# First block of a spectral filter and MLP: even and odd sums on array quarters, and a second scratch for its last rows

## The chip, the cores and the metric

The kernel runs on one core of one Trainium2 chip. The metric is the device time of one execution in microseconds. Lower is better. The core has TensorE (PE, with its weight loads PEld), VectorE (DVE), ScalarE (ACT), GpSimd (POOL) and SyncE (SP, which here only issues DMAs); DMAs are issued from SP, ACT and POOL.

## The reference

Two stages in float32; the weights of the second arrive as float64 and are converted on the chip.

```python
X = np.fft.rfft(x, axis=1)                       # x: 8 batches x 3008 rows x 256 columns
y = np.fft.irfft(X * (filt_r + 1j * filt_i), n=3008, axis=1)
t = y.reshape(24064, 256)                        # tokens
h = t @ w_in                                     # 256 -> 2048
g = h * np.clip(h + 3.0, 0.0, 6.0) / 6.0
out = g @ w_out                                  # 2048 -> 256
```

## The kernel before

*The transform.* 3008 = 47 x 64. A batch goes through four kinds of products: over 47 rows to 24 residues k (`a0_unit` for batch 0, `a_unit` after), over 64 to the frequencies of a residue (`b_unit`), times the filter on DVE (`f_unit`, `y_unit`), back over 64 (`bi_unit`), and back over the 24 residues to tokens (`n_first`, `n_five`, `n_unit`). Between `bi_unit` and the last step the values cross through a scratch in DRAM, `g_tmp` (`g_d`), since residues have to move from the columns of a tile to its partitions: `g_store` writes them from POOL, and `t4_load` or `first_load` reads them into the tile `t4`. The unit of the early work is a pair of residues i; `bi_unit(0, i)` treats the two pairs i and i + 1, so four residues, and batch 0 has such units at i = 0, 2, 4, 6, 8 and 10.

*Tokens.* A row j of tokens (47 of them) and the row 64 - j are made from the same values: one is the sum, the other the difference of an even and an odd part. The tile `xn` keeps both: index 0 and 1 of its third axis.

*The MLP.* The tokens go in blocks of 512, eight steps of 256 hidden columns to a block. Block 0 takes plain products (`plain_up`, `relu`, `hswish`, `plain_down`); later blocks take seven products for eight, which need sums of weights: `w_sums` on POOL, `w_scale` on ACT. Those sums start when the 15th of the 16 weight parts is converted.

*The weights.* Each of the 16 parts of the weights is loaded as integers (`load_bits`), split by ACT (`w_abs`) and put together by six DVE instructions (`w_conv`, `w_conv_2`; `convert(n)` does n whole parts). The buffers of the raw bits are borrowed from later tiles ("o", "g", "x").

*The first block.* It holds the rows j = 6 to 1 of batch 0 and their mirrors, 282 pairs, of which 256 are the block. To begin early, its last four residues (units i = 10 and 11) don't cross the scratch: `direct` multiplies the filtered spectrum `y` by a table `direct_t` that goes from frequencies to tokens. The other twenty residues come from `t4` in `n_first`, which adds its products to the same PSUM tiles (`psn`, and `po2`, `po3` for row j = 1) and copies the result to `xn` on ACT. Rows of the last unit that can still arrive in time (i = 8) are stored by `g0_first`, only the twelve that the block needs, from ACT and SP.

*Order.* The order of instructions on each engine is written out by hand: up to `n_first` and the first conversions in straight code at the end of the kernel, then by a plan of places (`at`) in each step. An engine's queue is worked off in this order. The framework puts in the waits. DMAs issued from SP and ACT take eight completion semaphores in turn, those from POOL eight others, and a DMA waits until the one before it on its semaphore has landed.

The ends of this order, before:

```python
        first_load(KH - 3 * TC, KH - TC)
        for i in 1, 2:
            w_abs(i)
        direct(NU - 2)
        direct(NU - 1)
        bi_unit(0, NU - 2, [...])
        ...
        n_first()
        g_store(0, NU - 4)
        g_store(0, NU - 2)
        ...
        w_abs(3)
        convert(3)
```

Of the kernel before, what the change touches and what calls it, by code (L numbers as in the profile page):

```python
# [26 lines left out]
N = 3008  # L27
# [27 lines left out]
RING = 3 * PAIRS  # L55
ND = (NJ + 1) * TOK
NX = PAIRS - NJ * NA
ATOM = 2 * KH
# [20 lines left out]
def _make_tables():  # L79
# [64 lines left out]

    def first_of(x, n):
        if n < NJ:
            return np.concatenate(x)
        return np.concatenate([x[0][:NX], x[1][:NX], cs_of([x[0][NX:], x[1][NX:]])])
# [5 lines left out]
    first = np.zeros((P, NJ + 1, TOK))  # L154
    last = np.zeros((P, NJ + 1, TOK))
    direct = np.zeros((P, TC, ND))
    for k in range(KH):
        for j in range(HC):
            for (ri, hh), x in terms(k, j, rows).items():
                if j in FIRST:  # L160
                    first[hh * 64 + ri * 32 + k, FIRST.index(j)] = first_of(x, FIRST.index(j))
# [16 lines left out]
    wai = np.concatenate([t.reshape(P, -1) for t in (groups, ones, first, last)], axis=1)  # L178
    f = np.float32
# [4 lines left out]
def kernel(  # L184
# [123 lines left out]
    def w_load(i, q):  # L308
        if W_AT[i] == "g":
            t = gp.tile([P, 7, 256], FP32, name="g")  # L310
            st["rest"] = t[:, 4:7, :].rearrange("p a n -> p (a n)")
            t = t.bitcast(I32)[:, 0:4, :].rearrange("p a n -> p (a n)")
# [346 lines left out]
    def first_load(k0, k1):  # L659
        for h in range(2):  # L660
            for ri in range(2):
                p0 = h * 64 + ri * 32
                nc.sync.dma_start(t4[p0 + k0:p0 + k1, 0:NJ + 1, :],
                                  g_d[0, ds(h * HC + 1, NJ + 1), ri, k0:k1, :].rearrange("j k d -> k j d"))
# [56 lines left out]


    def direct(i):
        if "psn" not in st:
            st["psn"] = {(c, dh): (psO.tile([P, 2, 2, P], FP32, name="po%d" % (2 + dh)).rearrange("p a u m -> p (a u m)")
                                   if c else psF.tile([P, 512], FP32, name="psn", tag="f"))
                         for c in range(2) for dh in range(2)}
        for u in range(2):
            k = 2 * i + u - KH + TC
            for (c, dh), ps in st["psn"].items():  # L730
                t, n = c * NJ * TOK, (1 if c else NJ) * TOK
                nc.tensor.matmul(ps[:, 0:n], st["y", 0, i][:, u, ts(dh, P)], st["direct"][k][:, ds(t, n)],
                                 start=k == 0, stop=False, skip_group_check=True)

    def n_first():
        for (c, dh), ps in st.pop("psn").items():
            for q, j in enumerate(chunks[c][1]):
                strips(ps[:, ts(q, TOK)], t4[:, j - 1, ts(dh, P)], edges[:, FIRST.index(j), :], start=False, stop=True)
            to = xn[:, dh, :, 0:PAIRS]
            if c == 0:  # L740
                nc.scalar.activation(out=to[:, :, 0:NJ * NA].rearrange("p h (j a) -> p j h a", a=NA),
                                     in_=ps[:, 0:NJ * TOK].rearrange("p (j h a) -> p j h a", j=NJ, h=2), func=AXT.Copy)
                continue
            nc.scalar.activation(out=to[:, :, NJ * NA:], in_=ps[:, 0:2 * NX].rearrange("p (h a) -> p h a", h=2), func=AXT.Copy)
            nc.scalar.activation(out=xn[:, dh, :, ds(PAIRS, NA - NX)],
                                 in_=ps[:, 2 * NX:TOK].rearrange("p (c a) -> p c a", c=2), func=AXT.Copy)

# [232 lines left out]
    with tc.manual_schedule():  # L980
# [65 lines left out]
        st["direct"] = [last[:, ts(k, ND)] for k in range(3)] + [st["rest"][:, 0:ND]]  # L1046
        nc.sync.dma_start(st["direct"][3], direct_d[:, 3, :])
        nc.sync.dma_start(edge, wai_d[:, ds(NW, ND)])
        load_bits(4)
        turn(0)  # L1050
        for c in range(NT):
# [99 lines left out]

        at(n_at[TAIL - 2] + 1, lambda: nc.sync.dma_start(edge, wai_d[:, ds(NW + ND, ND)]))
        at(LAST * NP + 3, b12_back)
# [136 lines left out]
```

## Time and profile before

| | us |
|---|---|
| median of 3 runs (2607.19 to 2607.8) | 2607.3 |
| span of the profiled execution, first to last instruction | 2607.0 |
| PE busy | 2591.8 |
| DVE busy | 2053.9 |
| first products of batch 0 on PE | 6.6 |
| `direct` on PE | 51.2 to 59.7 |
| `n_first` on PE | 61.6 to 63.8 |
| first product of the MLP | 64.2 |
| POOL's weight sums | 120.6 to 150.2 |

Times in the profile are in us from the first instruction; a line of a timeline gives start, duration, engine, source line, operation, output tile <- input tiles, shape and count, and in brackets the idle time of that engine before it and what ended it. A float32 product shows as two MATMUL records. "L765" is the helper `strips`, which all products on halves of the array's columns go through, so tile names tell them apart. The chain of waits is followed back from the last instruction, so each of its pieces is what the next one waited for. The span stands for the profiled execution's own time; it lies 0.3 us under the median.

### The profile page before, as it was taken

The numbers are of one execution on the slowest core, as the hardware profiler recorded it, in microseconds if no ns is written. First come the engines' busy times: TensorE is split into PE (matmuls) and PEld (weight loads), VectorE is DVE, ScalarE is ACT, GpSimd is POOL, SyncE is SP. The second block draws the span as 40 slices with busy tenths as digits, with TensorE's granted clock in tenths as the row PEclk, the third lists the DMA queues.
The fourth block names the chain that finished last, engine by engine and source line by source line (L and its number), as shares of the span: only waits on it lengthen the run. The fifth ranks groups of instructions, "written<-read, shape, count | busy, mean of one in ns | idle before, by whom it ended". The sixth has DMA issues, their size and how long they took to land.

```text
span 2607.0 us, 86613 instructions
## 1 busy us (share of the span) xinstructions
PE 2591.8 (99%) x37708; PEld 2051.0 (79%) x37708; DVE 2053.9 (79%) x3611; ACT 1295.6 (50%) x2677; POOL 486.7 (19%) x711
## 2 busy tenths in 40 slices
PE   8999999999999999999999999999999999999999
PEld 6487777878778787788877888777877778888887
DVE  7978868888788877888778887788877888766666
ACT  4554454545545455444554444545445454455554
POOL 2242021121211202111031210311113120111110
PEclk9999999999999999999999999999999999999999
DMA  8732234112241132411224112331123321110000
GB/s 247 224 92 81 59 101 119 54 33 87 74 123 54 33 87 78 119 54 37 83 83 114 54 38 82 89 108 54 54 66 91 106 57 49 50 44 24 20 22 26
DMA packets 130834, 200.32 MB, mean 77 GB/s; under 512 B 21602, under 2 KB 97472, under 8 KB 130262
## 3 DMA queue, kind: packets, MB, share of 16 engines
q1 hardware_dynamic: 115165, 150.12, 20.4%
q0 software_dynamic: 14720, 44.16, 6.1%
q8 instruction: 296, 4.85, 0.8%
q14 instruction: 84, 0.69, 0.1%
q10 hardware_dynamic: 569, 0.50, 0.1%
HBM read 122.43 MB, written 83.98 MB: 79 GB/s over the span
## 4 chain that ended last, share of the span: by engine, by line
PE 94%; DVE 3%; DMA 2%; POOL 1%; issue 0%; ACT 0%; SPq 0%; POOLq 0%; DVEq 0%; ACTq 0%
PE po L765 43%; PE al L765 24%; PE be L765 18%; PE psn L705 2%; PE psf L540 1%; PE psf L481 1%; PE psf L600 1%; PE be L600 1%; POOL w_all L369 1%; PE be L481 1%; DVE g L818 1%; DMA g_tmp<-t 1%; PE psf L765 0%; DMA ft<-in_filt_i_dram 0%; DVE y L335 0%
## 5 line engine op out<-in xcount | busy, mean ns | idle before, releaser
L765 PEld LDWEIGHTS po<-w_all,g 128*64 128x64 f32 x20808 | 1232.5, 137 | 247.0 <-issue 12.4
L765 PE MATMUL po<-w_all,g 128*64 128x128 f32 (+1 forms) x20808 | 1407.0, 274 | 1.4 <-DVE g L818 0.7
L813 ACT ACTIVATE r<-h,half_c 128x512 f32<-128x512 f32 x736 | 531.0, 722 | 346.7 <-DVE h L794 334.7
L765 PE MATMUL al<-xt,w_all 128*64 128x256 f32 x4416 | 664.0, 379 | 0.4 <-POOL w_all L369 0.3
L818 DVE SCALAR_TENSOR_TENSOR g<-r,h 128x512 f32<-128x512 f32 x736 | 536.2, 730 | 144.6 <-ACT r L813 129.2
L765 PE MATMUL be<-xt,w_all 128*64 128x256 f32 x2944 | 442.6, 379 | 0.0
L794 DVE TENSOR_TENSOR h<-be,s 128x512 f32<-128x512 f32 x368 | 253.8, 690 | 131.3 <-PE be L765 102.2
L760 POOL TENSOR_TENSOR xt<-xn 128x256 f32<-128x256 f32 x184 | 150.7, 838 | 890.3 <-ACT xn L687 890.3
L765 PEld LDWEIGHTS be<-xt,w_all 128*64 128x64 f32 x2944 | 211.3, 137 | 106.5
L765 PEld LDWEIGHTS al<-xt,w_all 128*64 128x64 f32 x4416 | 278.9, 137 | 1.7 <-POOL w_all L369 1.4
L808 ACT ACTIVATE h<-al 128x256 f32<-128x256 f32 x368 | 141.4, 384 | 273.2 <-PE al L765 272.4
L826 DVE TENSOR_TENSOR g<-g 128x512 f32<-128x512 f32 x367 | 261.4, 712 | 12.6
L799 DVE TENSOR_TENSOR h<-al,s 128x256 f32<-128x256 f32 x368 | 156.0, 424 | 135.6 <-PE al L765 130.5
L789 ACT ACTIVATE s<-al 128x256 f32<-128x256 f32 x368 | 141.6, 385 | 207.2 <-PE al L765 207.1
L765 PE MATMUL al<-xn,w_all 128*64 128x256 f32 (+1 forms) x1536 | 240.1, 393 | 1.1 <-DVE g L818 0.7
L765 PE MATMUL be<-xn,w_all 128*64 128x256 f32 (+1 forms) x1536 | 236.4, 388 | 0.0
L780 ACT ACTIVATE s<-be 128x256 f32<-128x256 f32 x368 | 141.4, 384 | 170.1 <-PE be L765 170.1
L825 DVE TENSOR_TENSOR g<-g 128x256 f32<-128x256 f32 x367 | 165.5, 451 | 12.6
L779 ACT ACTIVATE s<-al 128x256 f32<-128x256 f32 x368 | 141.5, 384 | 59.1 <-PE al L765 59.1
L831 DVE TENSOR_TENSOR g<-g 128x256 f32<-128x256 f32 x367 | 161.7, 441 | 2.4
L765 PEld LDWEIGHTS be<-xn,w_all 128*64 128x64 f32 x1536 | 110.3, 137 | 62.3 <-issue 7.4
L506 POOL DMA_DIRECT2D z_tmp<-t x144 | 72.0, 508 | 321.4 <-ACT s L780 296.0
(162 smaller groups left out, 1766.6 us busy)
## 6 DMA issues: line engine op xcount, KB each, us to landing
t<-g_tmp SPq DMA_DIRECT2D x184, 120.0 KB
t<-z_tmp SPq DMA_DIRECT2D x42, 512.0 KB
g_tmp<-t POOLq DMA_DIRECT2D x68, 256.0 KB, 4.3
z_tmp<-t POOLq DMA_DIRECT2D x120, 144.0 KB, 3.7
o_tmp<-o SPq DMA_DIRECT2D x46, 256.0 KB
xs<-in_x_dram SPq DMA_DIRECT2D x60, 192.0 KB
ft<-in_filt_r_dram SPq DMA_DIRECT2D x168, 64.0 KB
ft<-in_filt_i_dram SPq DMA_DIRECT2D x168, 64.0 KB
```

The lines of the kernel that those rows point to most:

```text
L760: nc.gpsimd.tensor_tensor(out=o, in0=x0, in1=x1, op=op_)
L765: nc.tensor.matmul(ps[ds(o, STRIP)], w[:, ds(o, STRIP)], x, skip_group_check=True, **kw)
L779: nc.scalar.activation(out=s[:, 0, :], in_=al, func=AXT.Copy)
L780: nc.scalar.activation(out=s5, in_=be[:, 1, :], func=AXT.Copy)
L789: nc.scalar.activation(out=s[:, 1, :], in_=al, func=AXT.Copy)
L794: nc.vector.tensor_tensor(out=st["h"][0].rearrange("p (a n) -> p a n", a=2), in0=be, in1=s, op=ALU.add)
L799: nc.vector.tensor_tensor(out=st["h"][1][:, 256:512], in0=al, in1=s5, op=ALU.add)
L813: nc.scalar.activation(out=r, in_=st["h"][i], func=AXT.Relu, bias=half_c, scale=1.0 / 6.0)
L818: nc.vector.scalar_tensor_tensor(out=st["g", k, p][:, o:o + 2, :].rearrange("p a n -> p (a n)"), in0=st["r", i], scalar=1.0, in1=st["h"][i ...
L825: v.tensor_tensor(out=g[:, G1, :], in0=g[:, G3, :], in1=g[:, G22, :], op=ALU.add)
L826: v.tensor_tensor(out=g[:, G3:G2 + 1:2, :], in0=g[:, G3:G1 + 1, :], in1=g[:, G11:G11 + 1, :].broadcast_to([P, 2, 256]), op=ALU.subtract)
L831: nc.vector.tensor_tensor(out=g[:, G4, :], in0=g[:, G12, :], in1=g[:, G2, :], op=ALU.subtract)
```

## The change

1. *Even and odd sums.* `direct` and `n_first` no longer compute both rows of a pair. A new helper `quarters` issues four products, for two halves of the rows (c: cosine and sine part) and two halves of the weight columns (g), each on 64 x 64 of the array. The cosine half gives the even part and goes to `psn`, the sine half the odd part and goes to `po2` or `po3`. The tables shrink to 282 columns for a residue and one table of 64 rows (`groups`, also used by `n_five`). After the products ACT copies the even part to `xn`, DVE adds and subtracts the odd part (two instructions of 128 x 256 for each half of the columns), and ACT copies the 26 pairs that belong to the next block.
2. *A second scratch.* The units i = 4, 6 and 8 are stored whole into `gf_tmp` (`gf_d`) by `gf_store`, from ACT, in halves of 64 rows (256 KB each), beside the store into `g_tmp` from POOL that stays. `gf_load` reads the rows of four residues with four DMAs of 24 KB; the twelve for three units stand together on SP after the loop. `first_load` fetches only the first eight residues, and `g0_first` goes. Unit 8's `g_store` stays behind `n_first` in the code.
3. *Order.* One conversion stands ahead of `n_first` and two behind it, where three stood behind it. The direct table is one load, and its last part no longer sits in a borrowed "g" buffer. Only the part of `t4` in use is cleared. The table reload in `wai_load` is two DMAs.

```diff
...
-            if j > 1:
+            if j:
...
-                    th = [2 * np.pi * ((fr * rows(j, h, a)) % N) / N for h in range(2)]
-                    direct[q, k - KH + TC, n * TOK:(n + 1) * TOK] = 2 / N * first_of(np.cos(th), n)
-                    direct[HALF + q, k - KH + TC, n * TOK:(n + 1) * TOK] = -2 / N * first_of(np.sin(th), n)
+                    th = 2 * np.pi * ((fr * rows(j, 0, a)) % N) / N
+                    direct[q, k - KH + TC, n * NA:(n + 1) * NA] = 2 / N * np.cos(th)
+                    direct[HALF + q, k - KH + TC, n * NA:(n + 1) * NA] = 2 / N * np.sin(th)
...
+    gf_d = nc.dram_tensor("gf_tmp", (3, NC, 2, TC, D), FP32, kind="Internal").ap()
...
-    def g0_first(i):
+    def gf_store(i):
         t = st["t3", 0, i]
         for v in range(2):
-            for h in range(2):
-                (nc.scalar, nc.sync)[v].dma_start(g_d[0, ds(h * HC + 1, NJ + 1), :, ds(2 * (i + v), 2), :].rearrange("c ri u d -> c ri (u d)"),
-                                    t[ds(v * 64 + h * HC + 1, NJ + 1)].rearrange("p ri u d -> p ri (u d)"))
+            nc.scalar.dma_start(gf_d[i // 2 - 2, :, :, ds(2 * v, 2), :].rearrange("c ri u d -> c ri (u d)"),
+                                t[ts(v, 64)].rearrange("p ri u d -> p ri (u d)"))
+
+    def gf_load(i, qs):
+        for h in range(2):
+            for ri in range(2):
+                qs[h].dma_start(t4[ds(ri * HALF + h * KH + 2 * i, TC), 0:NJ + 1, :],
+                                gf_d[i // 2 - 2, ds(h * HC + 1, NJ + 1), ri, :, :].rearrange("j k d -> k j d"))
...
+    def quarters(ps, dh, w, x, **kw):
+        for g in range(2):
+            for c in range(2):
+                nc.tensor.matmul(ps(c, dh)[ts(g, HALF)], w(c, ds(dh * P + g * HALF, HALF)), x(c), **kw)
...
-            for (c, dh), ps in st["psn"].items():
-                t, n = c * NJ * TOK, (1 if c else NJ) * TOK
-                nc.tensor.matmul(ps[:, 0:n], st["y", 0, i][:, u, ts(dh, P)], st["direct"][k][:, ds(t, n)],
-                                 start=k == 0, stop=False, skip_group_check=True)
+            for dh in range(2):
+                quarters(lambda c, dh: ps[c][dh][:, 0:NE], dh, lambda c, m: y[ts(c, HALF), u, m],
+                         lambda c: st["direct"][ts(c, HALF), ts(k, NE)], start=k == 0, stop=False, skip_group_check=True)
 
     def n_first():
-        for (c, dh), ps in st.pop("psn").items():
-            for q, j in enumerate(chunks[c][1]):
-                strips(ps[:, ts(q, TOK)], t4[:, j - 1, ts(dh, P)], edges[:, FIRST.index(j), :], start=False, stop=True)
-            to = xn[:, dh, :, 0:PAIRS]
...
+        ps = st.pop("psn")
+        for dh in range(2):
+            for q, j in enumerate(FIRST):
+                quarters(lambda c, dh: ps[c][dh][:, ts(q, NA)], dh, lambda c, m: t4[ds(c * HALF, ATOM), j - 1, m],
+                         lambda c: groups[ds(c * HALF, ATOM), j, :], start=False, stop=True, skip_group_check=True)
+            e, o = (xn[:, dh, c, :] for c in range(2))
+            odd = ps[1][dh]
+            nc.scalar.activation(out=e[:, 0:NE], in_=ps[0][dh][:, 0:NE], func=AXT.Copy)
+            nc.vector.tensor_tensor(out=o[:, 0:PAIRS], in0=e[:, 0:PAIRS], in1=odd[:, 0:PAIRS], op=ALU.add)
+            nc.vector.tensor_tensor(out=e[:, 0:PAIRS], in0=e[:, 0:PAIRS], in1=odd[:, 0:PAIRS], op=ALU.subtract)
+            nc.scalar.activation(out=o[:, PAIRS:NE], in_=odd[:, PAIRS:NE], func=AXT.Copy)
...
-        nc.gpsimd.memset(t4, 0.0)
+        nc.gpsimd.memset(t4[:, 0:NJ + 1, :], 0.0)
...
-        last = x0_at(HC * D - 2048, 3 * ND)
-        nc.sync.dma_start(last, direct_d[:, 0:3, :].rearrange("p k n -> p (k n)"))
+        st["direct"] = x0_at(HC * D - 2048, TC * NE)
+        nc.sync.dma_start(st["direct"], direct_d.rearrange("p k n -> p (k n)"))
+        nc.sync.dma_start(wai[:, NA:NA + NE], wai_d[:, NA:NA + NE])
         load_bits(3)
...
             if c:
                 bi_unit(0, 2 * c - 2)
-                (g0_first if c == NT - 1 else lambda i: g_store(0, i))(2 * c - 2)
-            if c == 4:
-                first_load(0, KH - 3 * TC)
-        first_load(KH - 3 * TC, KH - TC)
+            if c == NT - 2:
+                first_load(0, KH - 4 * TC)
+            if c > 2:
+                gf_store(2 * c - 2)
+            if 0 < c < NT - 1:
+                g_store(0, 2 * c - 2)
+        gf_load(NU - 8, (nc.sync, nc.sync))
+        gf_load(NU - 6, (nc.sync, nc.sync))
+        gf_load(NU - 4, (nc.sync, nc.sync))
...
+        convert(1)
         n_first()
...
-        convert(3)
+        convert(2)
...
-            nc.sync.dma_start(wai, wai_d[:, 0:NW])
+            for n0, n1 in (0, NA), (NA + NE, NW):
+                nc.sync.dma_start(wai[:, n0:n1], wai_d[:, n0:n1])
...
```

More of the change, by code (lines that the diff above doesn't have):

```diff
@@ L56 @@
 ND = (NJ + 1) * TOK
+NE = (NJ + 1) * NA
 NX = PAIRS - NJ * NA
@@ L143, in cs_of @@
         return np.concatenate([(x[0] + x[1]) / 2, (x[1] - x[0]) / 2])
[L145 to L148, printed above, removed]
     rows = np.vectorize(row, excluded=(0, 1))
@@ L153, in _make_tables @@
     ones = np.zeros((P, 2, TOK))
-    first = np.zeros((P, NJ + 1, TOK))
     last = np.zeros((P, NJ + 1, TOK))
-    direct = np.zeros((P, TC, ND))
+    direct = np.zeros((P, TC, NE))
     for k in range(KH):
@@ L159, in _make_tables @@
             for (ri, hh), x in terms(k, j, rows).items():
-                if j in FIRST:
-                    first[hh * 64 + ri * 32 + k, FIRST.index(j)] = first_of(x, FIRST.index(j))
                 if j < 2:
@@ L174, in _make_tables @@
                 for n, j in enumerate(FIRST):
-                    th = [2 * np.pi * ((fr * rows(j, h, a)) % N) / N for h in range(2)]
-                    direct[q, k - KH + TC, n * TOK:(n + 1) * TOK] = 2 / N * first_of(np.cos(th), n)
-                    direct[HALF + q, k - KH + TC, n * TOK:(n + 1) * TOK] = -2 / N * first_of(np.sin(th), n)
-    wai = np.concatenate([t.reshape(P, -1) for t in (groups, ones, first, last)], axis=1)
+                    th = 2 * np.pi * ((fr * rows(j, 0, a)) % N) / N
+                    direct[q, k - KH + TC, n * NA:(n + 1) * NA] = 2 / N * np.cos(th)
+                    direct[HALF + q, k - KH + TC, n * NA:(n + 1) * NA] = 2 / N * np.sin(th)
+    wai = np.concatenate([t.reshape(P, -1) for t in (groups, ones, last)], axis=1)
     f = np.float32
@@ L310, in w_load @@
             t = gp.tile([P, 7, 256], FP32, name="g")
-            st["rest"] = t[:, 4:7, :].rearrange("p a n -> p (a n)")
             t = t.bitcast(I32)[:, 0:4, :].rearrange("p a n -> p (a n)")
@@ L661, in first_load @@
             for ri in range(2):
-                p0 = h * 64 + ri * 32
+                p0 = ri * HALF + h * KH
                 nc.sync.dma_start(t4[p0 + k0:p0 + k1, 0:NJ + 1, :],
@@ L720, in n_unit @@
             ready(i)
+    def quarters(ps, dh, w, x, **kw):
+        for g in range(2):
+            for c in range(2):
+                nc.tensor.matmul(ps(c, dh)[ts(g, HALF)], w(c, ds(dh * P + g * HALF, HALF)), x(c), **kw)
     def direct(i):
         if "psn" not in st:
-            st["psn"] = {(c, dh): (psO.tile([P, 2, 2, P], FP32, name="po%d" % (2 + dh)).rearrange("p a u m -> p (a u m)")
-                                   if c else psF.tile([P, 512], FP32, name="psn", tag="f"))
-                         for c in range(2) for dh in range(2)}
+            st["psn"] = [[psO.tile([P, 2, 2, P], FP32, name="po%d" % (2 + dh)).rearrange("p a u m -> p (a u m)")
+                          if c else psF.tile([P, 512], FP32, name="psn", tag="f") for dh in range(2)] for c in range(2)]
+        ps = st["psn"]
+        y = st["y", 0, i]
@@ L735, in n_first @@
     def n_first():
-        for (c, dh), ps in st.pop("psn").items():
-            for q, j in enumerate(chunks[c][1]):
-                strips(ps[:, ts(q, TOK)], t4[:, j - 1, ts(dh, P)], edges[:, FIRST.index(j), :], start=False, stop=True)
-            to = xn[:, dh, :, 0:PAIRS]
[L740 to L746, printed above, removed]
+        ps = st.pop("psn")
@@ L1039 @@
             convert(j == 4)
-        nc.gpsimd.memset(t4, 0.0)
+        nc.gpsimd.memset(t4[:, 0:NJ + 1, :], 0.0)
         for c in range(FB, NT):
             table_load(0, c)
-        last = x0_at(HC * D - 2048, 3 * ND)
-        nc.sync.dma_start(last, direct_d[:, 0:3, :].rearrange("p k n -> p (k n)"))
+        st["direct"] = x0_at(HC * D - 2048, TC * NE)
+        nc.sync.dma_start(st["direct"], direct_d.rearrange("p k n -> p (k n)"))
+        nc.sync.dma_start(wai[:, NA:NA + NE], wai_d[:, NA:NA + NE])
         load_bits(3)
-        st["direct"] = [last[:, ts(k, ND)] for k in range(3)] + [st["rest"][:, 0:ND]]
-        nc.sync.dma_start(st["direct"][3], direct_d[:, 3, :])
-        nc.sync.dma_start(edge, wai_d[:, ds(NW, ND)])
         load_bits(4)
@@ L1150, in places @@
             return a_at, f_at, y_at, bi_at
-        at(n_at[TAIL - 2] + 1, lambda: nc.sync.dma_start(edge, wai_d[:, ds(NW + ND, ND)]))
+        at(n_at[TAIL - 2] + 1, lambda: nc.sync.dma_start(edge, wai_d[:, ds(NW, ND)]))
         at(LAST * NP + 3, b12_back)
```

## The prediction

> **What bounds the kernel now.** I read the page's parts 1 and 4 first, then the chain of waits near the start, because every line of the diff works in the first 80 us.
>
> ```profile
> span 2607.0 us, 86613 instructions
> PE 2591.8 (99%) x37708; PEld 2051.0 (79%) x37708; DVE 2053.9 (79%) x3611; ACT 1295.6 (50%) x2677; POOL 486.7 (19%) x711
> PE 94%; DVE 3%; DMA 2%; POOL 1%; issue 0%; ACT 0%; SPq 0%; POOLq 0%; DVEq 0%; ACTq 0%
> ```
>
> PE is the bound of the kernel as a whole. The 3% of DVE and the DMA and POOL shares are the first 140 us, and only there can the change act. The chain between 49 and 70 us:
>
> ```profile
> 50.98 4.56 DMA g_tmp<-t
> 55.56 2.31 DMA g_tmp<-t
> 58.19 3.34 DMA t<-g_tmp
> 61.62 1.86 PE psn L765 x40
> 64.22 1.94 PE al L765 x8
> 68.64 0.69 DVE g L818
> 69.33 0.35 DVE y L333
> ```
>
> The end of the transform for the first block is a chain of small DMAs: rows are stored, a second store waits for the first, they are loaded again, and `n_first` starts on PE when the load has landed, at 61.6. From 68.64 on the chain is DVE. DVE's timeline shows why:
>
> ```profile
> 63.60 0.43 DVE L337 TENSOR_SCALAR y<-y 128x512 int32<-128x512 int32 x1
> 65.64 0.69 DVE L354 TENSOR_TENSOR y<-g,y 128x512 f32<-128x512 f32 x1 [1.61 <-ACT g L324]
> 67.81 0.69 DVE L818 SCALAR_TENSOR_TENSOR g<-r,al 128x512 f32<-128x512 f32 x1
> 69.24 0.42 DVE L333 TENSOR_SCALAR y<-xt 128x512 int32<-128x512 int32 x1
> 119.77 0.69 DVE L361 SCALAR_TENSOR_TENSOR w_all<-s,y 128x512 f32<-128x512 f32 x1
> 120.95 0.69 DVE L818 SCALAR_TENSOR_TENSOR g<-r,al 128x512 f32<-128x512 f32 x1 [0.49 <-ACT r L813]
> ```
>
> No row of DVE between 65.64 and 119.77 carries an idle note: it converts weights and makes the first block's activations back to back. What hangs on its end is POOL's run of weight sums, and PE waits for those:
>
> ```profile
> 120.61 29.57 POOL L369 TENSOR_TENSOR w_all<-w_all 128x128 f32<-128x128 f32 x51 [15.89 <-DVE w_all L361]
> 139.46 0.65 PE L765 MATMUL al<-xt,w_all 128*64 128x256 f32 x4 [0.28 <-POOL w_all L369]
> ```
>
> So one mark decides: the conversion that DVE begins at 69.24, after the first two activations. What moves it moves POOL's start at 120.6 and PE at 139.5 by as much. An earlier PE alone gains nothing.
>
> **The change part by part.** *Products on quarters.* `direct` now issues 32 products of 64 rows, 64 columns of weights and 282 moving columns, where it issued 16 on the whole array:
>
> ```profile
> 51.16 1.81 PE L732 MATMUL psn<-w_all,t 128*128 128x470 f32 x4 [1.02 <-ACT t L587]
> 59.22 0.58 PE L732 MATMUL po<-g,t 128*128 128x94 f32 x4
> 95.15 1.38 PE L705 MATMUL psn<-wai,t 48*64 48x47 f32 x80
> ```
>
> Before, they take 51.16 to 59.7, 8.5 us. The four 470-column records follow each other in 1.6 us, two products, so 282 columns take 0.48. The third row is the same quarter form in `n_five`: ten groups of four products in 1.31 us, 0.13 for a group of 47 columns, so the four do run side by side. Eight groups cost 3.9 us; side by side not at all, 15.4. This gain of 4.6 us I cost at nothing: unit 11 of the spectrum is ready on DVE only at 54.65, so `direct` ends near 56.7, the last inverse products (1.1 us, 59.73 to 60.8 before) near 57.9, and then `n_first` waits for its loads.
>
> *The loads of `n_first`*, whose landing I call L (61.5 before). By the order of the built program:
> - `gf_store(4)` goes from ACT at 42.4 (the copy before POOL's store at 42.65). The eight completion semaphores of SP's and ACT's DMAs are taken in turn, and each DMA waits for the one before it on its semaphore. The direct table (issued at 36.6 before) and its neighbour on SP now wait for the two halves of `gf_store(4)`, and two weight loads of 512 KB stand behind them. So 1.75 MB that moved before 48.5 now start near 46. The table is needed at 51.2; lands near 50, hidden; ACT's second weight split needs its load by 58, hidden too.
> - `gf_store(8)` goes from ACT when both copies of unit 8 are done: 50.9 in both kernels, since PE runs without a gap up to these products. The copies used to wait until 49.8 for a store to land (longest wait of ACT on DMA 1.9 us) but PE ends the products only at 50.1. It stores 2 x 256 KB, where the old kernel stored 4 x 24 KB. ACT took 0.74 to 1.34 us for an issue, so the second half starts near 52. POOL's own store of unit 8, 512 KB, which waited until 62, goes at the same time.
> - Landing of such 256 KB stores: the rows issued at 33, 38, 42 and 48 took 4.8, 8.3, 6.3 and 3.7 us (least 2.9, most 9.7). DMA is busy with the delayed loads, so I take 5.4, between the last two: 57.4. Bounds 54.9 and 61.7.
> - The fourth row load of `gf_load(4)` waits on the semaphore of the first half, and all eight of `gf_load(6)` and `gf_load(8)` come after the second half on the one queue: seven more issues at 0.49 (four took 2.05) give 60.8. Landing 2.31 (the lone 24 KB store at 55.56) to 3.34 (the load at 58.19): L = 63.6. Bounds 60.3 and 68.6.
>
> *From L to the mark.* PE starts 0.09 after L (61.53 to 61.62); six groups of 0.13 for the first half, 0.79; ACT 0.24 behind (62.45 to 62.69) copies 282 columns, 0.41 between the 0.38 of 256 and the 0.57 of 470. Then DVE adds and subtracts, 128x256 with PSUM, 0.42 each (L799) at a step of 0.46: 2.5 us after L. ACT's small copy of the tail waits for that subtract, and the second half's large copy stands behind it in ACT's queue: 0.1 and 0.41, then two more on DVE: 3.9 after L. Only then come the two conversions that the change put behind `n_first`: 54.68, 58.52, 62.36 are the starts of three before, 3.84 each, so 7.68; then the two activations, 0.60 each. The mark is at L + 12.77.
>
> Before `n_first` DVE now has one conversion, 54.68 to 58.5, and stands still until L + 1.6, 6.7 us; the old order filled that with conversion and lost 1.61. The mark moves from 69.24 to 63.6 + 12.77 = 76.37, 7.1 later. Bounds with L: +3.8 and +12.1. Even with all rows there when PE is free at 57.9 it would be +1.4, since the four sums and the wait between them outweigh the 1.61.
>
> *Small parts.* The clearing of `t4` halves on POOL at 7 us, long before use; one DMA more in the table reload, about 0.4 us of SP at 72, and its rows are read by `n_five` at 95; the sums for the tail use the same table size. Nothing, covered by those distances. ACT's two issues of 1.0 after 42.4 push the copy at 44.15 by 0.3; PE needs it at 46.28.
>
> *An idle PE.* PE now stands for some 5.6 us before `n_first` and about 4.6 before the second step, since that waits for the first activation. The first matmuls of the kernel were slow:
>
> ```profile
> 3.02 3.78 PE L1028 MATMUL al<-r 128*128 128x512 f32 x4 [3.02 <-ACT r L1022]
> ```
>
> 0.95 for a record of 512 columns, when later ones follow at 0.43. Between 10 and 2600 us no gap is longer than about 1 us, so nothing shows whether it comes back. Bounds: nothing, and half speed for the first half of `n_first` (+0.8) and for the second step (about +1.5 past DVE's slack). I take nothing.
> The Trainium skill, "TensorE: Matmul & The Clock Gate", Part 1, says that PE falls to half its clock after an idle window of about 3.4 us and needs as long to come back; the granted clock in the profile is 1.00 even in 2.5 to 6.5 us, so that column would not show it. By the rule the sum would be some 1 to 2 us higher, as an estimate.
>
> *Sum.* Span 2607.0 + 7.1 = 2614.1; the profiled execution lies 0.3 below the median 2607.3, so 2614.4.
>
> **The rivals.** *A, likeliest:* as summed, L between 61.7 and 66, +5.2 to +9.5: 2612.5 to 2616.8. For it: three rings of 0.5 to 1.75 MB at the moment of the last store. Chance 0.53.
> *B, not slower:* the last store lands fast and L is below 61.7, where the shift falls under 0.2% (5.2 us, about what a measurement here tells from no change). The mechanism is the delayed loads: if they are through by 51, the store takes 2.9 to 3.7, L is 60.3 to 61.1, and the time 2611.1 to 2611.9. It decides at a landing before 55.5. For it: 1.75 MB at the 350 to 430 GB/s of 40 to 48 us need 4.5 us, about 46 to 51. Against it: another 2 MB of stores share that time. Chance 0.22.
> *C, dearer:* the store takes over 7 us, or PE restarts slowly: +9.5 to +14, 2616.8 to 2621.3. For it: the 8.3 at 38 us and the slow first records. Chance 0.21.
> *D, the quarters don't run side by side:* `direct` ends near 63.5, which L hides, and `n_first` takes 3.7 instead of 1.6, +1 to +2: inside A and C. Against it: the `n_five` row.
> *E, faster:* something later in the kernel gains, by a new rotation of the DMA semaphores. PE idles only some 6.5 us in all after 200 us. Chance 0.04.
>
> **How the numbers follow.** The prediction is A, 2614.4. The range takes A, the upper half of B and the near part of C: 2610.0 to 2619.0, leaving about 0.2. Slower by over 0.2%: A and C, 0.74; within: B, 0.22; faster: 0.04.
>
> **What would show it.** Right: DVE idle 5 to 8 us before the first of four new 128x256 sums, `n_first` on PE at 62 to 66, the direct table's load issued near 46 instead of 36.6, and POOL's sums starting at 124 to 131 instead of 120.6. Wrong: row loads landed before 60, DVE's conversions with a gap of their own that absorbs the shift, or POOL's start unmoved.

## The result and the profile after

The changed kernel takes 2626.3 us (median of 4 runs, 2623.9 to 2627.7) against 2607.6 for the old one beside it. The ratio is 1.0070, 95% interval 1.0056 to 1.0084: 18.7 us slower, where 7.1 were predicted. A second series, the last of the experiments below, gave 2624.9 us and 1.0064 (1.005 to 1.0077).

The page of the changed kernel: span, busy times, and the shares of the chain that ended last.

```profile
span 2623.4 us, 86795 instructions
PE 2591.5 (99%) x37788; PEld 2052.5 (78%) x37788; DVE 2055.2 (78%) x3615; ACT 1294.2 (49%) x2675; POOL 485.8 (19%) x711
PE 96%; DMA 2%; DVE 1%; issue 0%; SPq 0%; ACT 0%; ACTq 0%; POOL 0%; POOLq 0%; DVEq 0%
```

PE is busy for as long as before (2591.8), so the 16.4 us by which the span grew are time in which PE stands still. POOL has left the chain: its weight sums are no longer what PE waits for. The chain of waits of the changed kernel between 43 and 73 us (start, duration, what; "SPq" and "ACTq" are issues on those queues) shows where the first wait comes from:

```profile
43.76 0.58 ACTq L617
44.38 7.94 DMA gf_tmp<-t
52.33 0.32 SPq L1048
52.70 1.80 SPq L310
54.55 0.96 SPq L310
55.75 7.65 DMA t<-g_tmp
63.42 0.24 SPq L623
...
67.04 3.52 DMA t<-gf_tmp
70.65 0.41 PE psn L724 x2
```

Read it from the top. ACT issues the two halves of unit 4's scratch store; the second lands after 7.94 us, at 52.33. Only then does SP issue its small edge load (L1048) and, behind it, two weight loads of 512 KB (L310). Only behind these does `first_load` go, at 55.75, and it takes 7.65 us beside them. On the row loads of `gf_load(4)` SP waits 2.2 us for the second weight load to land and then for `first_load`, so it sends the third of them only at 63.42; the other row loads stand behind these, and the last one that PE waits for lands at 70.56, 9.0 us later than the rows before (61.53). The last scratch store, of unit 8, which the prediction took for the deciding one, is not in the chain at all.

The timeline of the same kernel on DVE, PE and POOL (in brackets the idle time before, and what ended it):

```profile
72.93 0.42 DVE L747 TENSOR_TENSOR xn<-xn,po 128x256 f32<-128x256 f32 x1 [12.96 <-ACT xn L746]
82.81 0.68 DVE L821 SCALAR_TENSOR_TENSOR g<-r,al 128x512 f32<-128x512 f32 x1
84.00 0.42 DVE L326 TENSOR_SCALAR y<-xt 128x512 int32<-128x512 int32 x1
73.95 3.68 PE L768 MATMUL al<-xn,w_all 128*64 128x512 f32 x8 [0.22 <-DVE xn L748]
83.54 2.44 PE L768 MATMUL al<-xn,w_all 128*64 128x512 f32 x8 [3.94 <-DVE g L821]
92.17 1.89 PE L768 MATMUL al<-xn,w_all 128*64 128x512 f32 x8
136.62 37.37 POOL L362 TENSOR_TENSOR w_all<-w_all 128x128 f32<-128x128 f32 x64 [15.17 <-DVE w_all L354]
```

DVE stands still for 12.96 us before the first sum, with two conversions still to do (75.2 to 82.8), and PE's second step waits 3.94 us for the activation behind them. The three PE rows are the first products of steps one, two and three. The same eight records take 3.68, 2.44 and 1.89 us. The windows of the changed kernel say why (start and end, length, busy time of PE, PEld, DVE, ACT and POOL with their counts, granted clock of PE, where 1.00 is full speed, DMA share, GB/s):

```profile
60.00:64.00 4.00, 0.00 (x0) 0.00 (x0) 0.00 (x0) 2.17 (x4) 1.12 (x2) 1.00 0.70 245
64.00:66.00 2.00, 0.00 (x0) 0.00 (x0) 0.00 (x0) 0.00 (x0) 0.01 (x1) 0.59 0.96 235
70.00:74.00 4.00, 3.13 (x98) 3.01 (x99) 0.84 (x2) 0.51 (x3) 0.00 (x0) 0.50 1.08 364
74.00:78.00 4.00, 4.00 (x10) 1.25 (x12) 3.41 (x7) 2.04 (x6) 0.00 (x0) 0.50 1.01 237
...
84.00:88.00 4.00, 4.00 (x14) 1.26 (x12) 3.76 (x8) 0.92 (x2) 0.00 (x0) 0.60 0.10 18
```

PE's clock falls to half while PE waits, and stays there until 78. It falls once more at the second step (0.60 in 84 to 88).

A better mark than the prediction's is the **third step**: the start of the last of the three PE rows, 92.17 against 75.49 before. In the old kernel the second and the third step start so:

```profile
68.55 1.94 PE L765 MATMUL al<-xn,w_all 128*64 128x512 f32 x8 [0.68 <-DVE g L818]
75.49 1.89 PE L765 MATMUL al<-xn,w_all 128*64 128x512 f32 x8
```

From the third step to the end of the span is 2530.9 to 2531.8 us in all fourteen profiled executions of this study, so whatever moves the third step moves the end, and nothing after it matters. The 16.7 us by which it is later, in three stretches:

| stretch | before | after | later by | predicted |
|---|---|---|---|---|
| start to landing of the rows | 61.53 | 70.56 | 9.0 | 2.1 |
| landing to second step on PE | 7.02 | 12.98 | 6.0 | 5.1 |
| second to third step | 6.94 | 8.63 | 1.7 | 0 |

(The predicted 5.1 is that of landing to the conversion at 69.24, 7.71 before and 12.77 foretold; DVE starts it 0.69 us after the second step in the old kernel and 0.46 after it in the changed one.) Some 1.4 of the 9.0 is already there when the spectrum starts: the first filter products are at 29.02 instead of 27.65 us. That moves from one execution to the next: 27.65, 27.73 and 28.32 in three kernels with the old products, 27.74 to 29.83 in ten with the new ones (an eleventh, with 30.91, has two loads moved to the start), 29.83 in the second profile of this same kernel. No run here separates what of it belongs to the change.

### The profile page after: what moved, and what is told of

Its sections match the earlier page's. It is cut to its first block, busy times and chain, and to the rows that moved or that the text cites. A ratio compares the mean times of both kernels' runs of the same rounds, so it can differ in the third digit from the quotient of the medians.

```text
span 2623.4 us, 86795 instructions
## 1 busy us (share of the span) xinstructions
PE 2591.5 (99%) x37788; PEld 2052.5 (78%) x37788; DVE 2055.2 (78%) x3615; ACT 1294.2 (49%) x2675; POOL 485.8 (19%) x711
## 4 chain that ended last, share of the span: by engine, by line
PE 96%; DMA 2%; DVE 1%; issue 0%; SPq 0%; ACT 0%; ACTq 0%; POOL 0%; POOLq 0%; DVEq 0%
PE po L768 44%; PE al L768 25%; PE be L768 18%; PE psn L703 2%; PE psf L533 1%; PE psf L474 1%; PE psf L593 1%; PE be L593 1%; PE be L474 1%; DMA ft<-in_filt_i_dram 0%; PE psf L768 0%; DMA wa<-wb_t 0%; PE psf L447 0%; DMA w_all<-in_x_dram 0%; DMA gf_tmp<-t 0%; DMA t<-g_tmp 0%
```

## The experiments

Two theories stood at the start. **Queue** (S in the expectations): the rows are late because SP's edge and weight loads wait for unit 4's store and the row loads stand behind them. **Last store** (W): the prediction's, the landing of unit 8's store sets the rows. Beside them, two smaller costs: the order of the conversions, and the slow PE.

**The old way of the rows, with the new products.**

```diff
-            if c == NT - 2:
-                first_load(0, KH - 4 * TC)
-            if c > 2:
-                gf_store(2 * c - 2)
-            if 0 < c < NT - 1:
-                g_store(0, 2 * c - 2)
-        gf_load(NU - 8, (nc.sync, nc.sync))
-        gf_load(NU - 6, (nc.sync, nc.sync))
-        gf_load(NU - 4, (nc.sync, nc.sync))
+                (g0_first if c == NT - 1 else lambda i: g_store(0, i))(2 * c - 2)
+            if c == 4:
+                first_load(0, KH - 3 * TC)
+        first_load(KH - 3 * TC, KH - TC)
```

> Changed kernel with the old way of the rows: no scratch of 64-row halves; units 4 and 6 go to the table by POOL's store and are loaded from there, the last unit by the four small stores, so nothing ahead on SP waits for a store from ACT. The products on quarters, the four sums on DVE and the order of the conversions stay as changed. Theory S (the direct table and the weight loads wait on SP for the second half of the scratch store of unit 4, and the row loads queue behind them): the landing of n_first's rows comes back from 70.6 to 61.5-63 us, the conversion that starts at 84.0 starts near 74-76, and the time falls from 2626 to 2613-2617, 5 to 10 us over the old kernel. What is then left is the order of the conversions (about 5) and what a waiting PE loses (1 to 2). Theory 'not the loads' (the cost sits in the sums and the slow PE alone): 2622 or more. The prediction's own rival W (the store of unit 8 alone sets the landing) also expects the low time here; the POOL run tells S from W.

Measured: 2614.1 us (10 runs), ratio 1.0022 (1.0012 to 1.0031). The rows land at 60.59, the third step is at 81.06, 5.6 later than before. So 11 to 12 of the 17 to 19 us belong to the new way of the rows, and about 6 to the new products with their order.

**The other half alone: the old kernel with the new way of the rows** (its layout of `t4` kept).

```diff
-                (g0_first if c == NT - 1 else lambda i: g_store(0, i))(2 * c - 2)
-            if c == 4:
-                first_load(0, KH - 3 * TC)
-        first_load(KH - 3 * TC, KH - TC)
+            if c == NT - 2:
+                first_load(0, KH - 4 * TC)
+            if c > 2:
+                gf_store(2 * c - 2)
+            if 0 < c < NT - 1:
+                g_store(0, 2 * c - 2)
+        gf_load(NU - 8, (nc.sync, nc.sync))
+        gf_load(NU - 6, (nc.sync, nc.sync))
+        gf_load(NU - 4, (nc.sync, nc.sync))
```

> Old kernel with only the way of the rows changed: three units' rows through the scratch of 64-row halves, loaded on SP; products on the whole array, no sums on DVE, and the old order of conversions (two ahead of n_first, one behind). The other half of the change alone. If the loads and the order of the conversions are separate costs, the rows land near 69 to 71 here too, DVE has converted two weights by then and has one left, and the third step on PE comes 13.96 us after the landing as before (75.49 against 61.53) plus 0.7 to 2.5 for a slow PE: 84 to 87, 8.5 to 11.5 later than before, time 2616.5 to 2619.5. If the products on quarters are what makes the rows late or PE slow: 2612 or less.

Measured: 2621.2 us, ratio 1.0051 (1.0037 to 1.0064), third step at 88.53: 13.3 us slower, some 2 more than the upper end expected. Its timeline on PE:

```profile
61.13 1.84 PE L738 MATMUL psn<-g,t 128*128 128x470 f32 x4 [0.48 <-DMA g<-direct_t]
73.12 3.40 PE L771 MATMUL psn<-wai,t 128*64 128x94 f32 x40 [8.71 <-DMA xt<-in_moe_w_in_dram]
```

The old direct tables are twice the size, 846 and 282 KB instead of one of 564, and they stand in the same delayed queue: `direct` itself now waits for its second table until 61.1, and `n_first` starts at 73.1, 2.5 us later than in the changed kernel. (The weight load in the last bracket is the profile's inference; `n_first` reads no weight bits, and what it waits for are the rows.) The halves 6.0 (old loads) and 13.3 (new loads alone) add up to 19.3 against 17.2 to 18.7 for both. The two costs are separate to within 2 us; that the smaller table takes a little off the queue's cost would fit the rest, but was not tested.

**The scratch stores from POOL instead of ACT.**

```diff
-            nc.scalar.dma_start(gf_d[i // 2 - 2, :, :, ds(2 * v, 2), :].rearrange("c ri u d -> c ri (u d)"),
+            nc.gpsimd.dma_start(gf_d[i // 2 - 2, :, :, ds(2 * v, 2), :].rearrange("c ri u d -> c ri (u d)"),
```

> Changed kernel with the stores to the scratch issued by POOL instead of ACT; same bytes, same loads from the scratch, same products and order. The direct table's load and the two weight loads on SP then wait for no store and are issued near 37-40 us again instead of 46.9-54.6. Theory S (what made n_first's rows late is SP's queue standing behind the store of unit 4): rows land near 62-65 instead of 70.6, time 2616 to 2620. Theory W (the landing of the last whole-unit store, unit 8, sets it, as the prediction had it): rows land at 68 or later, time 2624 to 2628.

Measured: 2616.3 us, ratio 1.0033 (1.002 to 1.0046), rows at 63.46, third step at 84.80. The chain of waits of this kernel:

```profile
52.75 0.53 POOL gf_tmp L617
53.28 5.16 DMA gf_tmp<-t
58.50 0.24 SPq L623
...
59.50 3.97 DMA t<-gf_tmp
63.55 0.31 PE po L724
```

This is the chain that the prediction had: the store of unit 8, landed after 5.16 us (predicted 5.4), then the row loads. Its numbers fit too, rows at 63.46 (63.6) and time 2616.3 (2614.4). In this kernel the last store is the limit, but with the stores on ACT the queue stands above it. The theory "last store" expected no change here and falls for the changed kernel.

**Only the two weight loads taken out of SP's queue.** First from the start of the queue on POOL:

```diff
-        load_bits(3)
-        load_bits(4)
+        load_bits(3, nc.gpsimd)
+        load_bits(4, nc.gpsimd)
```

> Changed kernel with only the two 512 KB weight loads moved from SP's queue to POOL's; the stores to the scratch stay on ACT, and the direct table's load and the 226-column edge load still wait on SP for the store of unit 4. Theory S in its narrow form (SP's queue order): the first row load follows the edge load at 52.6 instead of 55.75 us, and the two loads no longer share the DMA engines with it (they go near 40), so the rows land 3 to 6 us earlier than 70.6: 64.5 to 67.5, time 2626 - 3 to 6 = 2620 to 2623. If the delay came from the stores' bytes and not from the queue: rows at 70 or later, 2625 or more.

Measured: 2625.7 us, but with 2621.8 to 2627.4 in four runs; inconclusive as a time. In the profiled execution (2621.8) the rows land at 67.62. POOL issues the two loads at 8.2 and 9.1 us there, beside the loads that start the kernel, and the first filter products slip to 30.91, 1.9 us behind the changed kernel's. A second version has the two loads behind POOL's first store:

```diff
+            if c == 2:
+                load_bits(3, nc.gpsimd)
+                load_bits(4, nc.gpsimd)
             if c == NT - 2:
```

> As the run with the two weight loads on POOL, but issued there behind POOL's first store, near 35 to 37 us, so that they no longer share the DMA engines with the start (where the first run's table landed 1.9 us late, at 30.8 instead of 28.9). By SP's queue order the first row load goes 3 us earlier against the table's landing, and the rows land 4.8 us earlier, as in that run: near 66, time 2626 - 3.5 to 5.5 = 2620.5 to 2622.5. If the queue order isn't it, the rows land at 70 and the time stays at 2625 to 2627.

Measured: 2620.3 us (2618.8 to 2623.4), ratio 1.0050 (1.0037 to 1.0062), against 2624.9 for the changed kernel in the same series: 4.7 us. The chain of waits of this kernel:

```profile
47.17 0.52 ACTq L617
47.72 8.20 DMA gf_tmp<-t
55.93 4.01 DMA t<-gf_tmp
59.96 0.29 SPq L623
...
60.98 3.00 DMA t<-gf_tmp
```

`first_load` goes at 48.6 instead of 55.8, and the store that decides is the next one, unit 6's, landing after 8.2 us. The rows land at 63.99, 6.6 us earlier, with an early start of the spectrum (27.74) in part of it. Same stores, same engine, same bytes from the scratch: what was taken away is what stood in SP's queue. The two weight loads also ran earlier here, so the run does not separate their place in the queue from the share of the DMA engines that they took beside `first_load`.

**All conversions ahead of `n_first`.**

```diff
-        convert(1)
+        w_abs(3)
+        convert(3)
         n_first()
...
-        w_abs(3)
-        convert(2)
```

> Changed kernel with the third weight split and all three conversions ahead of n_first on DVE's and ACT's lists, so that DVE converts while it waits for the rows. By the prediction's sum, two conversions of 3.84 us stand behind n_first; if they fill the 13 us that DVE stands still, the rows land at 70.6 as before, and the first activation comes at n_first's end: the mark that was at 84.0 comes 5 us earlier or more, unless the xt buffers or ACT's splits hold it. Time 2626 - 3 to 5 = 2621 to 2623. If the order isn't it (the sums of POOL wait for something else): 2625 to 2627.

Measured: 2619.0 us, ratio 1.0043 (1.0028 to 1.0058): 6 to 7 us faster than the changed kernel, more than the 3 to 5 expected. The rows land at 69.54, 1.0 earlier, which is the earlier start of this execution (27.79 against 29.02). The landing to the second step is 8.53 instead of 12.98. The size was off because the mark was: I had counted to the conversion on DVE (84.00 to 79.61), while the second step on PE no longer waits for any activation (it starts at 78.07) and the third then waits 0.63 for DVE.

**A PE that is kept at work.** Products that serve nothing, 25 ahead of `n_first` and 11 after the first step's; `filler(n)` issues n products of 128 rows and 256 columns into a PSUM tile that nobody reads:

```diff
+        filler(25)
         n_first()
...
             if k == 0:
                 plain_up(p)
+                if p == 0:
+                    filler(11)
```

> Changed kernel with products on PE that serve nothing: 25 of 256 columns ahead of n_first and 11 after the first step's products, so that PE works through most of the two waits (11.6 us and 3.9 us). The rows still land near 70.5. Theory 'a waiting PE comes back slow' (granted clock 0.60 in 62-79 us, records of the second step 2.44 and 2.91 us where they took 1.72 before): n_first's part shortens by 0.7, the second step by 1.7, time 2626 - 2 to 2.5 = 2623.5 to 2624. If the slow records have another cause, such as transfers: no change, 2625 to 2627.5.

Measured: 2622.6 us, ratio 1.0057 (1.0042 to 1.0072), 2.3 to 3.7 faster. A window of this kernel, with the columns as above:

```profile
62.00:79.00 17.00, 15.21 (x152) 10.21 (x151) 6.51 (x13) 4.24 (x10) 1.12 (x2) 0.90 0.79 214
```

The second step in its timeline on PE:

```profile
82.51 1.94 PE L768 MATMUL al<-xn,w_all 128*64 128x512 f32 x8
84.28 1.89 PE L768 MATMUL be<-xn,w_all 128*64 128x512 f32 x8
```

The clock is 0.90 in 62 to 79 us where the changed kernel has 0.60, and the second to the third step takes 6.94 us, as in the old kernel, instead of 8.63. From landing to ACT's first copy it is 1.35 instead of 1.95. (This execution also starts 1.1 us earlier, at 27.88, which is no part of these two stretches.) So the slow PE is the clock, not transfers, and it costs 1.7 + 0.6. The transfers still ran beside it (214 GB/s in that window).

**What the new products cost at their best.** Old way of the rows, two conversions ahead and one behind, the third weight's split early, and 11 products that serve nothing behind `n_first`:

```diff
-        for i in 1, 2:
+        for i in 1, 2, 3:
             w_abs(i)
...
-        convert(1)
+        convert(2)
         n_first()
+        filler(11)
...
-        w_abs(3)
-        convert(2)
+        convert(1)
```

> Changed products with the old loads, an order that suits the four sums, and a PE kept busy: two conversions ahead of n_first and one behind it, the split of the third weight ahead of the last unit's copies, and 11 products of 256 columns that serve nothing between n_first and the first step. DVE: conversions 54.7 to 62.5, sums to 65, one conversion to 69, activations; the mark at 70 to 70.5 against 69.24 before, the third step on PE near 76.6 against 75.49. Time 1 to 2 us over the old kernel: 2609 to 2610. If the PE still slows (granted clock below 1.00 in 62 to 79 us): 2611 to 2612. At 2614, no better than the old loads alone, the order and the clock would not be the rest of the loss. Below 2607 the quarters would have a gain of their own.

Measured: 2610.5 us (11 runs), ratio 1.0009 (1.0001 to 1.0018), third step at 77.94, granted clock 1.00 throughout. The mark on DVE is at 71.66, not 70 to 70.5, with a spectrum that starts 1.6 later than before in this execution (29.25). That is as near to the old kernel as the new products came: the time that PE saves in `direct` buys nothing, since DVE has the four sums on top of its conversions and is the one that PE waits for before the second step (0.72 us).

**The old kernel with the early split alone**, so that DVE loses the only idle time that its profile showed between 65.6 and 119.8 (1.61 us):

```diff
-        for i in 1, 2:
+        for i in 1, 2, 3:
             w_abs(i)
...
-        w_abs(3)
         convert(3)
```

> Old kernel with ACT's split of the third weight moved ahead of the last unit's copies, so that DVE loses its 1.61 us wait at 65.6 (released by that split). The first activation then waits for ACT's copy of PE's first product, 66.9 instead of 67.8, and the second for the second, 68.5 instead of 68.6: gain 0.1 to 1.0 us, time 2607 to 2608, not to be told from the old kernel.

Measured: 2608.5 us, ratio 1.0003 (0.9994 to 1.0012), third step at 74.61: no difference that can be told. No run of this study beats the old kernel.

**All three costs mended, the change's own scratch kept.** Stores from POOL, two conversions ahead and one behind, fillers of 17 and 11 products:

```diff
-            nc.scalar.dma_start(gf_d[...
+            nc.gpsimd.dma_start(gf_d[...
...
-        for i in 1, 2:
+        for i in 1, 2, 3:
             w_abs(i)
...
-        convert(1)
+        convert(2)
+        filler(17)
         n_first()
+        filler(11)
...
-        w_abs(3)
-        convert(2)
+        convert(1)
```

> The changed kernel with its own scratch kept and all three costs mended: stores to the scratch from POOL (rows near 63.5), two conversions ahead of n_first and one behind with the third weight's split early, and products that serve nothing ahead of n_first (17) and behind it (11) so that PE's granted clock stays at 1.00. DVE: sums 65 to 68, conversion to 71.7, mark near 73, third step on PE near 79.4 against 75.49 before. Time 2610.5 to 2613. If the three causes are the whole loss, it is 13 to 15 us under the changed kernel; if a fourth is at work, it stays at 2615 or more.

Measured: 2617.7 us, 5 more than expected and no better than the stores on POOL alone. The fault was in the fillers, as the chain of waits shows:

```profile
58.63 7.54 PE po L1036 x34
66.17 0.18 PE psn L724
...
67.71 4.95 PE po L1036 x22
72.66 1.87 PE al L768 x8
```

Seventeen products are 34 records and take 7.54 us, 0.44 a product: I had sized them by the record. They held `n_first` and then the first step back. With 8 and 5 instead:

```diff
-        filler(17)
+        filler(8)
         n_first()
-        filler(11)
+        filler(5)
```

> As the run with all three costs mended, but with 8 products that serve nothing ahead of n_first and 5 behind it. There one of them took 0.44 us, not the 0.22 they were sized by, so that 17 of them held n_first back to 66.2 us and 11 held the first step back to 72.7, some 2.7 us each. Now 3.5 us and 2.2 us: n_first starts when the rows land, near 63.5, the first step at 68, the activations end DVE's work at 73, third step on PE near 79.5 to 80.5. Time 2611 to 2613, which leaves 3 to 5 us of the 17 to 18.7; at 2616 or more, the three causes are not the whole loss.

Measured: 2612.1 us (11 runs), ratio 1.0015 (1.0006 to 1.0024), third step at 77.70. The timeline of DVE in this kernel:

```profile
62.66 0.69 DVE L354 SCALAR_TENSOR_TENSOR w_all<-s,y 128x512 f32<-128x512 f32 x1
63.98 0.42 DVE L747 TENSOR_TENSOR xn<-xn,po 128x256 f32<-128x256 f32 x1 [0.63 <-ACT xn L746]
65.47 0.42 DVE L747 TENSOR_TENSOR xn<-xn,po 128x256 f32<-128x256 f32 x1 [0.62 <-ACT xn L746]
70.03 0.68 DVE L821 SCALAR_TENSOR_TENSOR g<-r,al 128x512 f32<-128x512 f32 x1
```

The 12.96 us of idle time are down to 0.63. Three causes, the queue, the order and the clock, are together 13 to 14 of the 17 to 19 us. Alone, the stores on POOL, the order and the fillers took off 8.6 to 10.0, 5.9 to 7.3 and 2.3 to 3.7 us, more in sum than together, so their gains overlap. The 4 that stay were not taken apart; the four sums are still on DVE's path, with two waits of 0.6 us for ACT between them.

**The changed kernel once more.**

> The changed kernel once more, beside the others on the same chip: how far its rows' landing (70.6) and its start (28.9) move from one profiled execution to the next. 2624 to 2628; landing 69 to 71.5.

Measured: 2624.9 us (2624.0 to 2625.9). The landing is at 71.19, the third step at 92.48; the first filter products at 29.83. The chain runs through the same unit 4 store (7.95 us) and the same weight loads; here the row loads wait for the second of them (8.92 us) and not for `first_load`.

## Why the prediction was right and wrong

*Right: the direction and the place.* The kernel is slower, the loss lies before the third step, and it comes from DVE and PE standing still until the rows land and from two conversions behind `n_first`. Rivals "not slower" and "faster" did not come.

*Right: the products on quarters.* The groups of four in the second unit's `direct` follow each other at 0.24 us a record, 0.48 a product, as estimated, so they do run side by side, and the rival that they don't falls. That the gain on PE is worth nothing held in the best version too.

*Right: landing to mark.* Predicted 12.77 us, measured 13.44 in the changed kernel (0.6 to 0.7 of it the slow clock, below), 12.60 with the old loads and 13.17 with the stores on POOL. The order and the sums were sized well.

*Wrong, at no cost to the number: the path behind the mark.* The prediction led it through POOL's weight sums to PE at 139.5. POOL's start did move, from 120.61 to 136.62, but in the changed kernel PE no longer waits for POOL, where it waited 0.28 us before: the path goes from the first activation straight to PE's second and third step.

*Wrong: the landing, 63.6 predicted and 70.56 measured; this is 7.0 of the miss, of which up to 1.4 is the later start of the spectrum.* The step that failed is "1.75 MB that moved before 48.5 now start near 46", and with it that the rows' landing was led through unit 8's store alone. The waits were the right ones, but I let them all end near 46, 3.6 us after the store's issue. Unit 4's first half did land at 46.8, and the table's load went at 46.89. The second half took 7.94 us, so the edge load and the two weight loads went only from 52.33 on. In that stretch, among stores above all, the DMA engines moved only 179 GB/s while 0.81 busy:

```profile
44.00:50.00 6.00, 6.00 (x31) 3.59 (x31) 5.22 (x8) 2.28 (x4) 2.26 (x4) 1.00 0.81 179
```

My own list had 4.8, 8.3, 6.3 and 3.7 us for such stores; I weighed it for unit 8 alone and let unit 4 have the shortest. I then asked only whether the table and the weights would arrive in time for their users, not what stands behind them on SP. `first_load` does, and `gf_load(4)` waits for it. So the chain to the rows went through SP's queue, not through unit 8's store; that one also went later than I had it (53.53 against 50.9), since ACT waited 4.03 us for an earlier store before its copies, and had still landed before it was needed. The upper bound of 68.6 was too low for the same reason: it stretched the last store and left the queue out. (From their own terms the two bounds come to 60.6 and 68.5 instead of 60.3 and 68.6, which changes nothing.)
The Trainium skill, "DMA: Bandwidth & Descriptors", "Anatomy of one DMA — SWDGE (gpsimd) path", says in passing that DMA engines do not wait on semaphores and that any such wait stands on the issuing sequencer. This trace agrees: between the table's load (46.89) and the edge load (52.33) SP, the issuing engine here, issues nothing. So a wait on SP has to be priced by everything that stands behind it, not by its own user alone.

*Wrong: the idle PE taken as nothing.* I had PE's two waits at 5.6 and 4.6 us; they were 11.6 and 3.9. Its slow restart cost 0.6 to 0.7 in `n_first` and 1.7 at the second step, 2.4 in all, near the sum of the two bounds that I gave (0.8 and 1.5). The filler run shows it to be the clock. My remark that the granted clock's column would not show it was wrong; it shows 0.50.
The Trainium skill, "TensorE: Matmul & The Clock Gate", "Part 1: The HAM clock gate", has half clock after an idle window of about 3.4 us and full clock after a busy one; the estimate of 1 to 2 us that I worked out from it and set aside was nearer than my nothing. The drop in the changed kernel, 5.3 us after PE's last product, fits that rule; its way back, 7.4 us after work had begun, is longer than such a window. The run with the old loads does not: there waits of 1.62 and 0.28 us were enough (last section), and the measurement decides.

*Wrong: where the profiled execution stands.* I put it 0.3 us under the median by taking the span for its time. In most runs shown here the time is 1.7 to 2.0 us above the span, so the execution with a span of 2607.0 took about 2608.8 and lay 1.3 over the median, while the one of the changed kernel (2625.5) lay 0.8 under its own. The 0.3 in the sum rested on this reading and was small; but the two executions together make 2.1 us by which the medians differ more than the two profiles do, and that is scatter, no mechanism.

*Together*: 7.0 for the landing, 2.4 for the clock and 2.1 for the two executions are 11.5 of the 11.9 us by which the time was missed. The signs went the foretold way and too far: DVE idle for 12.96 us instead of 5 to 8, `n_first` at 70.65 instead of 62 to 66, POOL's sums at 136.62 instead of 124 to 131; only the table's load, at 46.89, was where it was put. Rival C named a slow store and a slow PE, but had the slow store at unit 8, and its +14 is short of the 18.7 measured.

## What to carry to other kernels

When a moved store makes a load wait, list everything that stands behind that load on its queue, and follow the latest of the store's pieces, not the first. Price stores by the rate that stores show in the same stretch, not by that of loads. And where a change makes PE wait for more than a microsecond or two, add the half clock behind the wait, or give the wait to work that can be moved there.

## What the runs showed of the hardware

- *The clock.* In the stretches of half a microsecond that were read it is 1.00 or 0.50, and between them only where it changes. In the changed kernel it fell at 64.4 us, 5.3 after PE's last product, and came back at 78.0, 7.4 after work had begun again; in the run with two loads on POOL behind its first store it fell 3.4 and 4.3 us after PE's last product. With the old loads a wait of 1.62 us and one of 0.28 (at 58.5 to 60.7) were enough: the clock fell at 61.9, with PE at work again since 60.7. Two of its windows:

```profile
61.50:62.00 0.50, 0.50 (x48) 0.50 (x43) 0.00 (x0) 0.34 (x1) 0.50 (x2) 0.93 1.00 389
62.00:62.50 0.50, 0.50 (x22) 0.41 (x14) 0.40 (x1) 0.07 (x1) 0.50 (x2) 0.50 1.17 400
```

So waits of under 2 us in all can bring the half clock, and the price falls on the work after them. In the old kernel waits of 0.8, 0.4 and 0.7 us, spread over 8 us, left it at 1.00. What decides between the two cases no run here shows.
- *Stores.* A 256 KB half stored from ACT took 3.1 us (43.76 to 46.81) and its twin, issued 0.6 us behind it, 7.9, both among other stores. Why the twins differ so much was not taken apart.
- *The start.* The first filter products moved by 2.1 us (27.74 to 29.83) between executions of kernels that issue the same loads up to there; why is open.
